# Retention and SwiGLU on one core: the q of jobs 4 to 7 turned by VectorE from blocks of 32 instead of by TensorE

## The chip, the cores and the metric

The kernel runs on one core of one Trainium2 chip. The metric is the device time of one execution in microseconds (us), the median of several runs. All values are float32.

## The reference

Two blocks follow each other. The first is a retention block (attention without softmax, with a decay that depends on the head), the second a feed-forward block with RMS norm and SwiGLU.

```python
batch, n_heads, seq, head_dim = (8, 8, 576, 64)
scores = scale * np.matmul(q, k.transpose(0, 1, 3, 2))
gamma = 1.0 - 2.0 ** (-5.0 - np.arange(H))
Dmat = np.where(rel >= 0, gamma[:, None, None] ** rel[None], 0.0)
attn = np.matmul(scores * Dmat[None], v)
x = attn.transpose(0, 2, 1, 3).reshape(4608, 512)
xn = x / np.sqrt(np.mean(x * x, axis=-1, keepdims=True) + 1e-06) * rms_g
g = xn @ w_gate                       # 512 x 1536
out = (g * (1 / (1 + np.exp(-g))) * (xn @ w_val)) @ w_out
```

## The kernel before

**Jobs.** The retention block is cut into 32 jobs: job `j` is one batch and one pair of heads (`jobs[j]`, numbered from 0; the words "jobs 5 to 8" of the change count from 1 and are jobs 4 to 7 here, all of batch 1). A job needs `qT` and `kT` (two heads x 64 dimensions on the 128 partitions, 576 positions along a row) and `k` and `v` with the positions on the partitions. A sequence of 576 is 4 full tiles of 128 positions and a tail of 64; the tails are loaded apart (`load_tails`, `TAILS`: heads 0 and 1, then heads 2 to 7, of batch 0 and of batch 1). Positions are worked in chunks of 64 (`L`).

**Steps of a job.** `T` is `turn` (make `qT` and `kT`), `V` is `scale_v` (decay factors on `v`), `S` is `slot`, which issues in this order: `values(j-1)` (product of weighed scores with `v`, line 379), `scores(j)` (292), `states(j)` (k times v per chunk, 315), `weigh` and `sums` (VectorE, lines 328 and 341), and `carried(j-1)` (the carried states times `qT`, 399, and the move of the finished result into `x`, lines 423 and 425). `C7` closes the last of the first eight jobs.

**The first eight jobs** (batches 0 and 1; `FIRST` = 8) run at the start of the kernel with little else to do for TensorE. In them both q and k are loaded with the positions on the partitions (`load_first`) and turned on TensorE: q by eight products with the identity (line 236), k by four transposes (230), the two tails by a transpose each (245). ScalarE copies the results out of PSUM (241, 252). The decay factor of q is applied late: VectorE multiplies it into the result on its way into `x` (425, table `gq`). **All later jobs** load q and k in blocks of 32 x 32 (`load_qk`, four DMAs for each), ScalarE scales q (line 259, table `gp`) and VectorE turns it with one instruction (264); their result is moved into `x` by ScalarE (423). In all jobs ScalarE scales `v` and its tail (273).

**The order is written out by hand.** Everything is issued in the order of the program text on each engine. `LOADS` lists the loads of the start; nearly all go to the DMA queue of SyncE (SP), some small ones to that of ScalarE (`act_table`, `act_tails`). Each load waits until the load eight before it has landed. `PLAN` is a list of steps: `T`, `V`, `S`, `C` as above; `Q` and `G` squares and their sums for the norm, `N`, `D`, `X` the norm of the first two blocks of 512 tokens; `w` and `a` steps of preparing the weights (VectorE and ScalarE: the weights are split into mantissa and exponent); `U` is `up_plain`, four products of 128x512 for tokens that are not yet done with combined weights (704); `P` and `F` prepare and fetch a later job; `W36` makes 36 halves of weights ready. From the first `U000` on, products of `up_plain` stand between all other steps, until the main loop over blocks of tokens begins.

The weights are prepared in `set_of(k)`, three rotating places inside the tile `ring`; the first `v`, `k` and `q` of batch 1 lie in the same tile.

The lines that matter to the order of a job:

```python
def slot(j, rest=True):
    if rest: values(j - 1)
    scores(j); states(j); weigh(j)
    if j < FIRST: sums(j)
    if rest: carried(j - 1)
```

and in `carried`, the move that depends on the kind of job:

```python
if j >= FIRST:
    nc.scalar.copy(out=o, in_=part)
    continue
nc.vector.tensor_tensor(out=o, in0=part, in1=gq..., op=ALU.mult)
```

In `values`, a one-element instruction on GpSimd (`tick`, line 386) stands between the last product of `values` and the first product of `carried`.

Of the kernel before, what the change touches and what calls it, by code (L numbers as in the profile page):

```python
# [10 lines left out]
F32 = mybir.dt.float32  # L11
U32 = mybir.dt.uint32
AF = mybir.ActivationFunctionType
ALU = mybir.AluOpType
P = 128
L = P // 2
SQ = 32
# [27 lines left out]
def kernel(  # L45
# [11 lines left out]
    nc = tc.nc  # L57
    B, H, S, D = q.shape
    NTOK, DM = out.shape
    DFF = moe_w_gate.shape[1]  # L60
    NHP = H // 2
    NF = DFF // P
    NC = S // L
    NFULL = S // P
    TAIL = S - NFULL * P
# [5 lines left out]
    NK = NH // 2  # L71
    NG = NH // 2
    FIRST = 2 * NHP
    EPS = 1e-6
    K0, K1 = 2.38924456, 0.703952253
    assert (D, DM, NHP * P) == (64, H * D, DM) and S % SQ == 0 and NTOK % U == 0
# [4 lines left out]
    raw = ctx.enter_context(tc.tile_pool(name="raw", bufs=1))  # L81
# [31 lines left out]
    gp = const.tile([P, NHP, 2], F32, name="gp")  # L113
# [37 lines left out]

    def load_qk(j):
        b, hp = jobs[j]
        for nm, src in (("q", q), ("k", k)):
            t = raw.tile([P, S // SQ, SQ], F32, tag=nm + "raw", name=f"{nm}raw_{j}")
            for e in range(2):
                rows = src[b, 2 * hp + e].rearrange("(t b) (i a) -> i b t a", b=SQ, a=SQ)
                for i in range(D // SQ):  # L160
                    r = e * D + i * SQ
                    nc.sync.dma_start(out=t[r : r + SQ], in_=rows[i])
            st[j][nm + "raw"] = t

    def load_first(j, nm):

        b, hp = jobs[j]
        n = NFULL * P
        at = (3 * hp + "qkv".index(nm)) * n
        room = (h_1.rearrange("p f t -> p (f t)") if b else flat_h)[:, at : at + n]  # L170
        src = {"q": q, "k": k, "v": v}[nm][b, 2 * hp : 2 * hp + 2, :n]
        if nm == "q":
            st[j]["q"] = room.rearrange("p (e t d) -> p e t d", e=2, d=D)
            nc.sync.dma_start(
                out=room.rearrange("p (e t) -> p e t", e=2),
                in_=src.rearrange("e (p t) d -> p e (t d)", p=P),
            )
            return
        t = st[j][nm] = room.rearrange("p (c e d) -> p c e d", e=2, d=D)
        for e in range(2):  # L180
            nc.sync.dma_start(out=t[:, :, e], in_=src[e].rearrange("(c p) d -> p c d", p=P))

    def load_tails(i, queue):

        b, heads = TAILS[i]
        for n, (nm, src) in enumerate((("qt", q), ("kt", k), ("vt", v))):
            at = NV + (3 * b + n) * DM
            t = vi[:TAIL, at : at + DM].rearrange("p (h d) -> p h d", d=D)
            cut = slice(heads[0], heads[-1] + 1)
            queue.dma_start(  # L190
                out=t[:, cut], in_=src[b, cut, NFULL * P :].rearrange("h p d -> p h d")
            )
            for hp in range(heads[0] // 2, heads[-1] // 2 + 1):
                st[b * NHP + hp][nm] = t[:, 2 * hp : 2 * hp + 2]
# [17 lines left out]
    def warm_up(n, width=P):  # L212
# [3 lines left out]
        for _ in range(n):  # L216
# [2 lines left out]
                start=True, stop=True,  # L219
            )  # L220

    def turn(j):

        d = st[j]
        n = NFULL
        for nm in "qk":
            ps = bank(f"turn_{j}_{nm}")
            for c in range(n):
                if nm == "k":
                    nc.tensor.transpose(  # L230
                        out=ps[:, c * P : c * P + P],
                        in_=d["k"][:, c].rearrange("p e d -> p (e d)"), identity=ident,
                    )
                    continue
                for e in range(2):
                    nc.tensor.matmul(
                        ps[side(e), c : n * P : n], lhsT=d["q"][:, e, c], rhs=ident,
                        start=True, stop=True,
                    )
            t = d[nm + "T"] = att.tile([P, S], F32, tag=nm + "T", name=f"{nm}T_{j}")  # L240
            nc.scalar.copy(out=t[:, : n * P], in_=ps[:, : n * P])
        last = bank(f"turn_{j}_t")
        for i, nm in enumerate("qk"):
            o = slice(i * TAIL, i * TAIL + TAIL)
            nc.tensor.transpose(
                out=last[:, o], in_=d[nm + "t"].rearrange("p e d -> p (e d)"),
                identity=ident[:TAIL, :TAIL],
            )
        warm_up(j == 0, 2 * P)
        for i, nm in enumerate("qk"):  # L250
            o = slice(i * TAIL, i * TAIL + TAIL)
            nc.scalar.copy(out=d[nm + "T"][:, NFULL * P :], in_=last[:, o])

    def prepare(j):

        d = st[j]
        for odd in range(2):
            t = d["qraw"][:, odd::2]
            nc.scalar.activation(
                out=t, in_=t, func=AF.Copy, scale=gp[:, jobs[j][1], odd : odd + 1]  # L260
            )
        for nm in ("q", "k"):
            t = att.tile([P, S], F32, tag=nm + "T", name=f"{nm}T_{j}")
            nc.vector.transpose(out=t, in_=d.pop(nm + "raw").rearrange("p t a -> p (t a)"))
            d[nm + "T"] = t
        scale_v(j)

    def scale_v(j):
        d = st[j]
        hp = jobs[j][1]  # L270
        for e in range(2):
            for t in (d["v"][:, :, e], d["vt"][:, e]):
                nc.scalar.activation(
                    out=t, in_=t, func=AF.Copy, scale=gv[: t.shape[0], hp, e : e + 1]
                )
# [115 lines left out]
    def carried(j):  # L391
# [15 lines left out]
        for u, c0, c1, o in ((b, 0, cut, b * L), (b + 1, cut, NC, 0)):  # L407
# [3 lines left out]
            for first in (c0, c0 + 1):  # L411
# [7 lines left out]
                for to, at in moves:  # L419
                    o = x[to, first - c0 :: 2]  # L420
                    part = av[odd][at, i * L : (i + n) * L].rearrange("p (c k) -> p c k", k=L)
                    if j >= FIRST:
                        nc.scalar.copy(out=o, in_=part)  # L423
                        continue
                    nc.vector.tensor_tensor(
                        out=o, in0=part, in1=gq[:, hp].unsqueeze(1).to_broadcast([P, n, L]),
                        op=ALU.mult,
                    )
# [722 lines left out]
    def store_blocks(n):  # L1151
# [4 lines left out]

    IN_PSUM = range(4, 36)
    PLAN = """
        T0 V0 a1 S0 a1 T1 a1 a1 V1 S1 T2 V2 F8 S2 V3 T3 w1 a1 w1 Q0 a1 a1 G0 Q1 a1 S3 T4 G1 V4
        a1 a1 w1 Q2 a1 S4 a1 V5 w1 T5 G2 V6 Q3 a1 a1 G3 a1 S5 w1 T6 V7 w1 Q4 a1 S6 N0 a1 w1 a1  # L1160
        D0 a1 a1 G4 a1 T7 a1 w1 a1 w1 a1 a1 a1 Q5 X0 G5 S7 w1 U000 w1 a1 a1 a1 Q6 a1 C7 G6 a1 Q7
        G7 U001 N1 w1 w1 w1 D1 U002 w1 a1 X1 a1 w1 a1 w1 w1 w1 w1 a1 a1 a1 w1 a1 U003 a1 w1 w1
        a1 U100 w1 a1 w1 U110 w1 a1 a1 w1 a1 w1 U101 a1 w1 w1 w1 a1 a1 a1 a1 a1 w1 U010 a1 U102
        a1 w1 a1 w1 w1 w1 U111 w1 U112 a1 a1 w1 w1 a1 a1 a1 w1 w1 a1 a1 w1 a1 U011 w1 U012 w1 w1
        a1 w1 a1 a1 U020 U021 w1 U103 w1 a1 a1 w1 w1 a1 a1 w1 w1 a1 U113 a1 w1 w1 a1 a1 a1 w1
        U013 a1 U022 a1 a1 a1 a1 w1 w1 a1 w1 U120 w1 a1 a1 a1 a1 a1 w1 U130 w1 w1 a1 a1 a1 U121
        a1 a1 a1 P8 a1 a1 w1 w1 a1 w1 U023 w1 U122 a1 F9 U123 w1 a1 w1 a1 w1 a1 a1 a1 w1 a1 w1
        w1 a1 a1 U030 U031 a1 a1 w1 w1 a1 a1 w1 a1 w1 U032 a1 U033 w1 U131 w1 w1 w1 w1 U132 a1
        w1 w1 P9 a1 a1 a1 a1 a1 a1 w1 w1 a1 U040 F10 a1 w1 a1 U133 w1 a1 U041 a1 a1 a1 w1 a1 a1
        U042 a1 w1 w1 w1 w1 w1 a1 a1 U050 w1 a1 a1 w1 a1 w1 a1 w1 w1 U051 U052 w1 w1 a1 w1 a1 a1  # L1170
        U140 w1 a1 a1 a1 w1 a1 w1 a1 a1 a1 w1 a1 U043 U053 W36 S8 P10 U141 S9 a1 U150 a1 U142
        F11 a1 a1 d0 a1 a1 Q8 z0 i0 a1 a1 U143 a1 S10 r1 a1 a1 U151 P11 U152 S11 U153 a1 d1 i1
        d2 a1 a1 a1 Q9 r2 A0 r99 A0 A0 j2 A0 G8 a1 a1 d3 b0 d4 C11 A0 i3 A0 d5 a1 A0 a1 F12 A0
        G9 b1 i4 Q10 k0 Q11 a1 b2 A0 i5 A0 a1 a1 G10 A0 j6 A0 A0 A0 a1 P12 A0 j7 b3 A0 j8 c2 A1
        c0 F13 A1 v1 A1 c3 A1 j9 o0 G11 A1 A1 j10 A1 A1 j11 A1 i12 A1 R2 A1 Y2 A1 X2 M2 p1 a1 a1
        i13 A1 A1 A1 A1
    """
    TAILS = ((0, range(2)), (0, range(2, H)), (1, range(2)), (1, range(2, H)))
    LOADS = [("k", 0), ("act_table", 2), ("q", 0), ("q", 1), ("q", 2), ("v", 0), ("k", 1), ("v", 1), ("tails", 1), ("q", 3), ("k", 2), ("act_table", 0), ("table", 3), ("half", 0), ("v", 2), ("v", 3), ("k", 3), ("v", 4), ("q", 4), ("k", 4), ("act_tails", 0), ("half", 1), ("tails", 2), ("k", 5), ("tails", 3), ("q", 5), ("v", 5), ("v", 6), ("q", 6), ("v", 7), ("k", 6), ("rms_g", 0), ("k", 7), ("q", 7), ("half", 2), ("half", 3), ("table", 4), ("half", 4)]
    stores = []  # L1180
    n_joined = 0
    due = False
# [160 lines left out]
```

## Time and profile before

| | |
|---|---|
| median of 3 runs | 1105.85 us (1105.76 to 1105.95) |
| the profiled execution's own time | 1103.84 us |
| its span, first to last instruction | 1102.0 us |
| TensorE (PE) busy | 1087.4 us, 99% of the span |
| VectorE (DVE), ScalarE (ACT), GpSimd (POOL) busy | 753.2, 339.5, 457.9 us |
| granted TensorE clock | 1.00 |

The profile names engines PE, PEld (its weight loads), DVE, ACT, POOL and SP. A float32 product appears as two records. A group line gives the source line, engine, operation, output<-inputs, shape and count, then busy time and mean duration in ns, then the idle time before these instructions and what ended it. "issue" as a releaser means that the profile shows nothing for which the engine waited. Times of day are microseconds from the start of the span.

### The profile page before, as it was taken

To read this page: it belongs to the slowest core of one execution; us is meant where nothing else is said; L and a number is where in the kernel's file an instruction comes from. 1 tells how busy PE (TensorE), PEld (TensorE's weight loads), DVE (VectorE), ACT (ScalarE), POOL (GpSimd) and SP (SyncE) were. 2 spreads that over 40 slices of the span, in tenths; PEclk is the share of its full clock that TensorE was granted. 3 is DMA by queue.
4 is the path that set the end of the run, shared out by engine and by line. 5 is a ranking of instruction groups with operands and counts; after the bars stand their busy time and mean duration, and the time that the engine had idled before them with its cause. 6 is when DMAs were issued, how large, how long until landed. Compare 5 with 4: busy or idle time off the path is not lost.

```text
span 1102.0 us, 24455 instructions
## 1 busy us (share of the span) xinstructions
PE 1087.4 (99%) x10102; PEld 912.5 (83%) x10102; DVE 753.2 (68%) x1219; ACT 339.5 (31%) x757; POOL 457.9 (42%) x421
## 2 busy tenths in 40 slices
PE   8899999999999999999999999999999999999998
PEld 7744444479988899889988998889888988898898
DVE  3878468878866794678667775668565935594467
ACT  5755564431124412342034303340233111211110
POOL 0027316548430195027702581238322942393236
PEclk9999999999999999999999999999999999999999
DMA  8856787696978876796678965888475855575461
GB/s 211 194 174 232 295 262 211 196 353 170 304 265 233 217 254 225 181 242 235 237 217 193 295 256 143 245 255 295 132 204 194 281 192 174 186 284 164 151 249 41
DMA packets 253871, 243.60 MB, mean 221 GB/s; under 512 B 193216, under 2 KB 213824, under 8 KB 247616
## 3 DMA queue, kind: packets, MB, share of 16 engines
q1 hardware_dynamic: 252320, 241.64, 69.3%
q8 instruction: 79, 1.29, 0.5%
q10 hardware_dynamic: 1440, 0.40, 0.2%
q14 instruction: 32, 0.26, 0.1%
HBM read 211.92 MB, written 30.08 MB: 220 GB/s over the span
## 4 chain that ended last, share of the span: by engine, by line
PE 96%; DVE 1%; DMA 1%; issue 1%; SPq 0%; ACT 0%; POOL 0%; POOLq 0%; DVEq 0%; ACTq 0%
PE up L704 15%; PE x L644 14%; PE w L644 13%; PE z L644 13%; PE y L644 7%; PE xo L814 6%; PE xp L814 4%; PE zo L814 4%; PE zp L814 3%; PE wo L814 2%; PE yo L814 2%; PE av L379 2%; PE wp L814 2%; PE av L399 2%; PE s L292 2%; PE yp L814 2%
## 5 line engine op out<-in xcount | busy, mean ns | idle before, releaser
L704 PE MATMUL up<-x,ring 128*128 128x512 f32 x384 | 167.1, 594 | 0.0
L644 PE MATMUL x<-x,ring 128*128 128x256 f32 x672 | 161.0, 382 | 0.0
L644 PE MATMUL w<-sums,ring 128*128 128x256 f32 x672 | 158.9, 379 | 0.0
L644 PE MATMUL z<-x,ring 128*128 128x256 f32 x672 | 158.7, 379 | 0.0
L766 POOL TENSOR_TENSOR vi<-h 128x384 f32<-128x384 f32 x32 | 39.9, 1247 | 275.3 <-DVE h L663 266.2
L704 PEld LDWEIGHTS up<-x,ring 128*128 128x128 f32 x384 | 72.2, 190 | 89.3 <-issue 84.7
L644 PEld LDWEIGHTS z<-x,ring 128*128 128x128 f32 x672 | 127.7, 190 | 19.9 <-issue 2.9
L644 PEld LDWEIGHTS w<-sums,ring 128*128 128x128 f32 x672 | 127.6, 190 | 17.4
L644 PEld LDWEIGHTS x<-x,ring 128*128 128x128 f32 x672 | 125.3, 190 | 17.5 <-ACT m L670 0.2
L771 POOL TENSOR_TENSOR vi<-h 128x384 f32<-128x384 f32 (+2 forms) x46 | 47.6, 1034 | 149.3 <-DVE h L663 149.3
L1010 POOL TENSOR_TENSOR vi<-vi 128x512 f32<-128x512 f32 (+1 forms) x77 | 78.1, 1027 | 38.2 <-DVE vi L841 21.5
L644 PE MATMUL y<-sums,ring 128*128 128x256 f32 x336 | 79.4, 379 | 0.0
L670 ACT COPY m<-x 128x512 f32<-128x512 f32 x42 | 24.6, 586 | 173.3 <-PE x L644 173.3
L651 DVE TENSOR_TENSOR h<-u,w 128x512 f32<-128x512 f32 x42 | 28.9, 688 | 67.8 <-PE w L644 67.8
L651 DVE TENSOR_TENSOR u<-m,y 128x512 f32<-128x512 f32 x42 | 28.8, 687 | 63.3 <-PE y L644 62.6
L644 PEld LDWEIGHTS y<-sums,ring 128*128 128x128 f32 x336 | 63.8, 190 | 8.7
L665 ACT ACTIVATE h<-h 128x512 f32<-128x512 f32 x63 | 39.7, 630 | 82.6 <-DVE h L651 82.6
L1130 POOL TENSOR_TENSOR vi<-vi 128x512 f32<-128x512 f32 (+1 forms) x24 | 40.7, 1696 | 30.7 <-DVE vi L1119 17.1
L651 DVE TENSOR_TENSOR u<-u,z 128x512 f32<-128x512 f32 x42 | 28.9, 688 | 33.5 <-PE z L644 33.4
L1130 POOL TENSOR_TENSOR ring<-ring 128x512 f32<-128x512 f32 x24 | 30.4, 1270 | 49.4 <-DMA w_up_blocks<-ring 43.7
L771 POOL TENSOR_TENSOR vi<-vi,h 128x384 f32<-128x384 f32 (+2 forms) x46 | 48.4, 1053 | 3.6
L423 ACT COPY x<-av 128x192 f32<-128x192 f32 (+6 forms) x136 | 37.7, 277 | 29.8 <-PE av L399 28.3
(314 smaller groups left out, 2087.3 us busy)
## 6 DMA issues: line engine op xcount, KB each, us to landing
ring<-w_out_blocks SPq DMA_DIRECT2D x59, 1344.0 KB, 6.7
ring<-w_up_blocks SPq DMA_DIRECT2D x42, 1792.0 KB, 7.7
w_out_blocks<-vi SPq DMA_DIRECT2D x21, 448.0 KB, 6.5
out_dram<-vi SPq DMA_DIRECT2D x64, 128.0 KB, 3.1
qraw<-in_q_dram SPq DMA_DIRECT2D x96, 72.0 KB, 4.8
kraw<-in_k_dram SPq DMA_DIRECT2D x96, 72.0 KB, 2.8
k<-in_k_dram SPq DMA_DIRECT2D x48, 128.0 KB, 2.8
v<-in_v_dram SPq DMA_DIRECT2D x48, 128.0 KB, 2.8
```

The costliest lines, as they stand in the source:

```text
L292: nc.tensor.matmul(s[e][side(odd), i * L : i * L + L], lhsT=d["kT"][side(e), c * L : c * L + L], rhs=d["qT"][side(e), c * L : c * L + L], ...
L423: nc.scalar.copy(out=o, in_=part)
L644: nc.tensor.matmul(ps[:, i * HU : i * HU + HU], lhsT=w[:, PLACE[blk], c, i * P : i * P + P], rhs=t_of[u][blk][:, c], start=(start and i == ...
L651: nc.vector.tensor_tensor(out=o, in0=a, in1=pairs_of(ps), op=ALU.add)
L665: nc.scalar.activation(out=o, in_=c, func=AF.Silu)
L670: nc.scalar.copy(out=s1, in_=pairs_of(x_))
L704: nc.tensor.matmul(ps, lhsT=w[:, PLACE[blk], c % 2, i * P : i * P + P], rhs=x_of[u][:, c], start=(c == 0), stop=(c == NHP - 1),)
L766: eng.tensor_tensor(out=i1, in0=x12, in1=x11, op=ALU.subtract)
L771: eng.tensor_tensor(out=o[:, c], in0=a[:, c], in1=b[:, c], op=op)
L814: nc.tensor.matmul(ps, lhsT=lhs[:, c], rhs=w[:, s, c], start=((nm, s // 4) not in first), stop=False, skip_group_check=True,)
L1010: eng.tensor_tensor(out=t[:, :, o], in0=t[:, :, x], in1=t[:, :, y], op=ALU.add)
L1130: nc.gpsimd.tensor_tensor(out=t[o], in0=t[x], in1=t[y], op=op)
```

## The change

For jobs 4 to 7, q is loaded by `load_qk` in blocks of 32 (into a free part of `ring`), scaled by ScalarE with `gp` and turned by VectorE (`turn_raw`); TensorE turns only k and its tail. The q tails of batch 1 are no longer loaded. The results of these jobs are moved into `x` by ScalarE without the factor `gq`. In all first eight jobs `qT` and `kT` become two halves of one tile, so that both tails are copied out of PSUM by one instruction; and the tails of `v` are scaled by four GpSimd instructions (one for each entry of `TAILS`) instead of 16 ScalarE instructions. `LOADS` and `PLAN` are written anew; `gp` moves to ScalarE's queue, `causal` and `gc` to SP's.

```diff
+    TURNED = range(4)
...
-    def load_qk(j):
+    def load_qk(j, names="qk"):
...
+            if j < FIRST:
+                at = AT_SETS + 4 * BLOCK * 3 - (FIRST - j) * S
+                t = ring[:, at : at + S].rearrange("p (t a) -> p t a", a=SQ)
...
     def load_first(j, nm):
+        if nm == "q" and j not in TURNED:
+            load_qk(j, "q")
+            return
...
     def load_tails(i, queue):
+            if nm == "qt" and b * NHP + heads[0] // 2 not in TURNED:
+                continue
...
+    def place_turned(j):
+        t = att.tile([P, 2, S], F32, tag="qkT", name=f"qkT_{j}")
+        st[j]["qT"], st[j]["kT"] = t[:, 0], t[:, 1]
+        return t
+
     def turn(j):
-        for nm in "qk":
+        both = place_turned(j)
+        names = "qk" if j in TURNED else "k"
+        if j not in TURNED:
+            turn_raw(j, "q")
+        for nm in names:
...
-        for i, nm in enumerate("qk"):
-            o = slice(i * TAIL, i * TAIL + TAIL)
-            nc.scalar.copy(out=d[nm + "T"][:, NFULL * P :], in_=last[:, o])
+        first = 2 - len(names)
+        nc.scalar.copy(
+            out=both[:, first:, NFULL * P :],
+            in_=last[:, : len(names) * TAIL].rearrange("p (i t) -> p i t", t=TAIL),
+        )
+
+    def turn_raw(j, names):
+        d = st[j]
+        if "q" in names:
+            for odd in range(2):
+                t = d["qraw"][:, odd::2]
+                nc.scalar.activation(
+                    out=t, in_=t, func=AF.Copy, scale=gp[:, jobs[j][1], odd : odd + 1]
+                )
+        for nm in names:
+            nc.vector.transpose(
+                out=d[nm + "T"], in_=d.pop(nm + "raw").rearrange("p t a -> p (t a)")
+            )
...
+    def scale_tails(b, heads):
+        cut = slice(heads[0], heads[-1] + 1)
+        t = vi[:TAIL, NV + (3 * b + 2) * DM : NV + (3 * b + 3) * DM]
+        t = t.rearrange("p (h d) -> p h d", d=D)[:, cut]
+        g = gv[:TAIL].rearrange("p h e -> p (h e)")[:, cut].unsqueeze(2)
+        nc.gpsimd.tensor_tensor(
+            out=t, in0=t, in1=g.to_broadcast([TAIL, len(heads), D]), op=ALU.mult
+        )
+
     def scale_v(j):
+        for b, heads in TAILS:
+            if (b, 2 * hp) == (jobs[j][0], heads[0]) and j < FIRST:
+                scale_tails(b, heads)
         for e in range(2):
-            for t in (d["v"][:, :, e], d["vt"][:, e]):
+            for t in (d["v"][:, :, e], d["vt"][:, e])[: 1 if j < FIRST else 2]:
...
-                    if j >= FIRST:
+                    if j not in TURNED:
                         nc.scalar.copy(out=o, in_=part)
...
-        T0 V0 a1 S0 a1 T1 a1 a1 V1 S1 T2 V2 F8 S2 V3 T3 w1 a1 w1 Q0 a1 a1 G0 Q1 a1 S3 T4 G1 V4
-        a1 a1 w1 Q2 a1 S4 a1 V5 w1 T5 G2 V6 Q3 a1 a1 G3 a1 S5 w1 T6 V7 w1 Q4 a1 S6 N0 a1 w1 a1
-        D0 a1 a1 G4 a1 T7 a1 w1 a1 w1 a1 a1 a1 Q5 X0 G5 S7 w1 U000 w1 a1 a1 a1 Q6 a1 C7 G6 a1 Q7
+        a1 V0 a1 a1 T0 S0 a1 T1 V1 S1 V2 T2 S2 T3 a1 w1 V3 a1 S3 a1 Q0 a1 G0 Q1 T4 a1 a1 V4 G1
+        w1 w1 a1 F8 a1 S4 Q2 a1 T5 V5 G2 V6 w1 Q3 G3 a1 a1 a1 a1 a1 S5 a1 w1 T6 w1 N0 a1 w1 Q4
+        w1 D0 S6 V7 T7 a1 a1 a1 Q5 X0 S7 G4 a1 a1 a1 a1 w1 Q6 a1 w1 a1 a1 U000 w1 a1 w1 G5 a1 C7
...
-    LOADS = [("k", 0), ("act_table", 2), ("q", 0), ("q", 1), ("q", 2), ("v", 0), ("k", 1), ("v", 1), ("tails", 1), ("q", 3), ("k", 2), ("act_table", 0), ("table", 3), ("half", 0), ("v", 2), ("v", 3), ("k", 3), ("v", 4), ("q", 4), ("k", 4), ("act_tails", 0), ("half", 1), ("tails", 2), ("k", 5), ("tails", 3), ("q", 5), ("v", 5), ("v", 6), ("q", 6), ("v", 7), ("k", 6), ("rms_g", 0), ("k", 7), ("q", 7), ("half", 2), ("half", 3), ("table", 4), ("half", 4)]
+    LOADS = [("k", 0), ("v", 0), ("q", 0), ("q", 1), ("table", 0), ("k", 1), ("v", 1), ("tails", 1), ("table", 2), ("q", 2), ("table", 3), ("v", 2), ("k", 2), ("v", 3), ("q", 3), ("k", 3), ("v", 4), ("k", 4), ("tails", 2), ("half", 0), ("q", 4), ("q", 5), ("half", 1), ("act_tails", 0), ("k", 5), ("v", 5), ("tails", 3), ("v", 6), ("q", 6), ("k", 6), ("half", 2), ("rms_g", 0), ("v", 7), ("k", 7), ("q", 7), ("half", 3), ("half", 4), ("act_table", 4)]
```

The rest of `PLAN` (the steps between `U001` and the main loop) holds the same `U`, `S`, `P`, `F`, `A` steps in another interleaving; of the inner sums, groups 2 and 6 move from VectorE to GpSimd and groups 3, 4 and 5 from GpSimd to VectorE.

## The prediction

> **What bounds the kernel now.** I read the engine totals first, then the windows on both sides of the first `up` product, then TensorE's groups and idle times in the early part, and last SP's queue.
>
> ```profile
> PE 1087.4 (99%) x10102; PEld 912.5 (83%) x10102; DVE 753.2 (68%) x1219; ACT 339.5 (31%) x757; POOL 457.9 (42%) x421
> ```
>
> TensorE is idle for only 14.6 us of 1102.0. Where these lie is told by two windows (columns: busy time of PE, PEld, DVE, ACT, POOL with counts, clock, DMA share, GB/s):
>
> ```profile
> 10.00:55.00 45.00, 38.98 (x1226) 33.48 (x1225) 33.05 (x87) 34.00 (x89) 1.64 (x8) 1.00 0.84 204
> 55.00:201.00 146.00, 145.72 (x415) 65.81 (x414) 105.41 (x182) 80.18 (x141) 59.58 (x43) 1.00 0.72 245
> ```
>
> Until 55 us (jobs 0 to 7, where the change lies) TensorE idles 6 us, DVE and ACT are three quarters busy and the DMA engines 84%: nothing bounds alone. From the first `up` at 55.05 us on TensorE never rests; after 195 us its waits add up to 1.6 us, and 4.3 us follow its last product. So **a change before 55 us is worth what it shifts the first `up`**, not what it takes off TensorE. In the early part, by shape, and TensorE's timeline at job 4:
>
> ```profile
> L236 PE MATMUL turn_q<-ident,ring 128*64 128x128 f32 x64 | 5.1, 281 | 2.9 <-issue 2.9
> ...
> L241 ACT COPY qT<-turn_q 128x512 f32<-128x512 f32 x8 | 4.7, 583 | 11.4 <-PE turn_q L236 11.4
> ```
> ```profile
> 27.47 0.65 PE L236 MATMUL turn_q<-ident,ring 128*64 128x128 f32 x6
> 29.71 0.81 PE L236 MATMUL turn_q<-ident,ring 128*64 128x128 f32 x10 [1.59 <-issue]
> ```
>
> The turn of q of jobs 4 to 7 is seen whole, with a pause of 1.59 us for which no wait is shown. SP's queue (start, duration, loads):
>
> ```profile
> 39.95 0.51 SPq L174 DMA_DIRECT2D ring<-in_q_dram  x1
> ...
> 43.27 3.93 SPq L162 DMA_DIRECT2D qraw<-in_q_dram  x4
> ```
>
> These are one q in the old and one in the new form: one issue against four. SP issues without a pause from 0.7 to 43 us. By the landing records q of job 7 lands at 43.98 us and is used at 47.4; q of job 5 lands at 34.98 and is used at 35.8. TensorE runs only 1 to 3 us behind the loads.
>
> **What the Trainium skill says.** "Runtime: NRT & Kernel Launch", section "Instruction fetch mechanics": instructions come in 16 KiB blocks by DMA, their cost "mostly hidden". Not here: packets of 16384 B start at 26.9 and 46.9 us, and TensorE pauses at 28.1 and 48.2; loads in flight land late too (in the gap around 31.8 us two successive landings are 2.85 us apart). "DMA: Bandwidth & Descriptors", table "Specifications": transfers under 512 B miss the line rate. The trace agrees: median packet 13 ns for 128 B, 18 for 256 B, 46 for 1024 B, so a byte of the new q costs 2.3 times a byte of the old. "GPSIMD Engine Reference", section 3.1: elementwise work is 1.96 times slower on GpSimd than on VectorE; here a 128x384 add takes 1.00 to 1.60 us against 0.55 to 0.86.
>
> **The change, step by step.** *TensorE:* eight q products per job are one stretch of 1.02 us (chain, jobs 5 and 6), the q tail half of 0.27: (1.02 + 0.13) x 4 = **4.6 us out**. That is the most the change can gain by its own work.
>
> *DVE:* out, the multiplies by `gq` of four jobs, four records and 0.94 us for each (first line, job 4), 3.8 us; in, four transposes of 128x576 (second line, of a later job):
>
> ```profile
> 42.01 0.94 DVE L425 TENSOR_TENSOR x<-av,gq 128x256 f32<-128x256 f32 x4
> ```
> ```profile
> L264 DVE STREAM_TRANSPOSE qT<-qraw 128x576 f32<-128x576 f32 x17 | 13.1, 772 | 0.7 <-PE av L399 0.7
> ```
>
> 4 x 0.77 = 3.1; net -0.7. *ACT:* out, four q copies (0.58), eight tail copies (0.22) and 16 tail scalings (0.34): 9.5 us. In, eight scalings
>
> ```profile
> L259 ACT ACTIVATE qraw<-qraw,gp 128x288 f32<-128x288 f32 x48 | 23.0, 530 | 8.5 <-DMA qraw<-in_q_dram 7.9 <-DVE sum L341 0.5
> ```
>
> 4.2, and 16 moves into `x`, 0.37 + 0.32 + 0.21 + 0.21 per job, 4.4: net -0.9. Neither engine is the bound; both small gains I count as nothing. *POOL:* four scalings, two 64x384 and two 64x128, by its own rows about 1.25 and 0.65 us. POOL is idle until 60 us (1.6 us busy), but behind such a scaling stands the `tick`, which releases `carried`. The late case is heads 2 to 7 of batch 1: v tail lands about 37.9 (ledger below), done 39.2, `carried(4)` due 39.4. Cost 0 to 0.5; I take 0.
>
> *Loads, the step that decides.* Old: four q of 256 packets of 1024 B (256 x 46 / 16 engines = 0.74 us) and 512 tail packets (0.58 in all): 3.5 us. New: 4 x 4 x 576 packets x 13 / 16 = 7.5 us. **4.0 us more** DMA time, and SP issues 16 q blocks for 4 q and 2 fewer tails. To see when it lands I add packet times in the order of `LOADS` and set landings of before against the sum: 20.4 landed at 27.7, 24.5 at 35.3, 28.7 at 39.9, 31.4 at 44.0, 34.1 at 47.3, 36.9 at 49.8 (job 8's first blocks, of the new kind). Instruction fetches are in these. In the new order the sums are: q4 20.4, q5 22.3, k5 24.8, last tails 26.4, q6 29.8, k6 31.0, k7 34.9, q7 36.7, so landings of about 27.7, 30.5, 35.5, 37.5, 42.2, 43.5, 48.4 and **49.7** against 43.98 for q7.
>
> TensorE behind it, with old durations: q4 27.7 + 1.06 + 0.77 = 29.5, so `scores(4)` at about 29.6 against 31.9, 2.3 ahead. k5 at 35.5 and the tails at 37.5 hold job 5: `carried(4)` ends 40.4 against 40.73. k6 at 43.5: turn 0.7, copies 0.8, scores, states and carried 2.0: 47.0 against 45.5. Norm 1.9, k7 turn 0.7, `rb` 1.05, values 0.67: 51.3. q7: 49.7 + 1.06 + 0.77 = **51.5**, which ends last. In before `scores(7)` at 52.62 stand 2.43 ahead of the first `up`; so 53.9 against 55.05, **-1.1 us**. Of 4.6 us, 3.5 turn into waits for loads.
>
> *The start:* q0 is issued behind v0, two issues, about +1.0; but `V0` moves ahead of the copies and `V1` no longer waits for its tail (states(1) idled 0.94 at 15.45): taken as 0, between -0.5 and +0.5. *After 55 us:* all products stay, in other order; groups 3 to 5 of inner sums go to DVE, 2 and 6 to POOL. Before has 0.7 us of waits between 200 and 260 us, so no gain beyond that; a plan that fits worse may cost up to 3. I take 0. The `ring` place of raw q lies under weight sets 1 and 2, the first of which is written after `x` of the second 512 tokens is normed, and its last reader is job 7's transpose.
>
> **Rivals.** (1) *The loads keep up*, nearly the whole 4.6 us is kept. For it: job 8's blocks landed 0.2 to 0.4 us apart, not 0.47, and fewer products mean fewer fetches. Against: other engines had been catching up behind a fetch. If 16 blocks take 0.3 each, q7 lands 2.7 earlier, 47.0; then k7 and TensorE's own order hold, first `up` near 51.5: -3.5, median **1102.3**. (2) *SP's queue becomes the bound, slower.* q7's last block is SP's 64th DMA, q7 was the 50th, issued at 39.95: 0.80 us each. At that rate it is issued at 51.1, lands 4.0 later at 55.1, first `up` at 55.1 + 1.83 + 2.43 = 59.4: +4.3, **1110.1**. It decides from a landing of q7 at 50.8 on. Against: 72 KB blocks free the eight places sooner, and part of the 0.80 is waiting for the engines. (3) *The new plan stalls TensorE after 55 us*, by +1 to +3: **1107**. (4) That the change does not do what it says: the instruction order of the changed kernel has 32 fewer q products, 4 fewer tail turns and 4 more transposes, so this has no weight.
>
> **How the numbers follow.** Against the profiled execution's 1103.84 the likeliest case gives 1102.7. The median is 2.0 higher; the same step there gives **1104.8**. About 0.2% (2.2 us) is what a measurement of this kernel can tell from no change. Main case, -2.2 to +2.2: 0.45. Loads keep up: 0.29 faster. SP's queue or the plan, beyond +2.2: 0.26. The range reaches from the full TensorE saving, less a little (-4.4, 1101.4), to most of the queue case (1109.5); its own range for the main case is 1103.6 to 1108.
>
> **What would show it.** TensorE's busy total near 1082.8. Idle before 55 us up from 6 to about 9.5 us, with waits for DMA (`kT`, tails) or for DVE's transpose ahead of jobs 5 to 7; a raw q7 landing of 49 to 51 us; first `up` near 53.9; no new waits after it. Wrong if q7 lands before 47.5 or after 52, if TensorE waits after 55 us grow beyond 1 us, or if ACT ends the waits early on.

## The result, and the profile after

The changed kernel takes 1108.02 us (median of 20 runs) beside 1104.96 for the kernel before on the same chip: ratio **1.0027, 95% interval 1.0016 to 1.0038**. It is slower by some 3 us, more than the 0.2% that the prediction set as a measurable difference; 1104.8 and "no change" were forecast. The profiled execution took 1106.24 us (before: 1103.84), its span is 1104.5.

The page gives the engine totals and the granted clock in 40 slices:

```profile
PE 1086.5 (98%) x10034; PEld 913.2 (83%) x10034; DVE 751.0 (68%) x1211; ACT 339.0 (31%) x753; POOL 452.7 (41%) x421
...
PEclk9699999999999999999999999999999999999999
```

TensorE issues 68 records of products fewer, yet its busy total is only 0.9 us lower, not 4.6: in the second slice (27.6 to 55.2 us) the clock stands at 6 tenths. The windows on both sides of the first `up` in the forecast (busy time of PE, PEld, DVE, ACT, POOL, then clock, DMA share, GB/s):

```profile
10.00:55.00 45.00, 38.14 (x1083) 33.39 (x1085) 30.42 (x77) 29.36 (x75) 3.64 (x11) 0.81 0.83 187
55.00:201.00 146.00, 145.72 (x502) 67.19 (x495) 108.23 (x181) 81.92 (x148) 59.75 (x43) 1.00 0.76 249
```

The clock was 1.00 in the first of these before, and is 0.81 now: the clock records show half rate from 30.2 to 43.85 us and from 47.27 to 50.68, in units of 3.413 us. The waits of TensorE (line, releaser: total, times, longest):

```profile
PE av L440 <- issue: 3.9, 3, 1.7
PE s L333 <- DVE qkT L286: 3.2, 2, 2.3
PE turn_q L257 <- DMA h<-in_q_dram: 2.6, 1, 2.6
PE av L420 <- issue: 1.9, 1, 1.9
```

and where they lie (start, busy, instructions, the idle time before them):

```profile
29.14 0.63 PE L420 MATMUL av<-ret,h 64*64 64x64 f32 x28 [1.92 <-issue]
32.27 1.34 PE L333 MATMUL s<-qkT 64*64 64x64 f32 x40 [2.34 <-DVE qkT L286]
37.24 0.91 PE L440 MATMUL av<-qkT,sum 64*64 64x64 f32 x12 [1.70 <-issue]
54.58 0.81 PE L333 MATMUL s<-qkT 64*64 64x64 f32 x40 [0.90 <-DVE qkT L286]
```

`scores` waits for VectorE's turned q at job 4 (32.27) and at job 7 (54.58). The clock record goes to half at 30.20 us, 1.06 us after the end of the pause of 1.92 and 0.27 us into the wait of 2.34. The products are slower then: the same 40 records take 1.34 us at 32.27 and 0.81 at 54.58. The second half-rate stretch, from 47.27 on, follows 3.4 us in which TensorE does not wait at all; over half of that time goes to sixteen records of one column each, of the norm:

```profile
44.90 1.95 PE L522 MATMUL ms<-mean_w,sq 128*128 128x1 f32 x16
```

The chain that ends in the first `up`:

```profile
49.66 1.48 PE av L440 x29
...
51.16 0.38 ACT x L464 x2
...
51.64 0.29 ACT x L464 x2
...
52.26 0.52 ACT ring L314
52.78 0.85 ACT ring L282 x2
...
53.66 0.79 DVE qkT L286
...
54.58 0.81 PE s L333 x40
...
55.86 0.93 PE av L440 x32
56.79 0.63 PE up L745
```

The last steps follow **ScalarE's order**: after `carried` of an earlier job come its moves into `x`, then the scaling of `v` (314), then that of q (282), then VectorE's turn, then `scores(7)`. Before, these jobs had neither the moves nor a scaling of q on ScalarE. But the wait that this order causes is 0.90 us, and the chain starts with a `carried` at half rate (1.48 us for 29 records). The first `up` stands at 56.72 us, against 54.98 before (the chain's figures, 56.79 here and 55.05 in the prediction, leave out what still overlaps with the work before).

By windows that end at the first `up`, TensorE was busy for 46.46 us and idle for 8.52 before; now it is busy for 46.02 and idle for 10.70. So the 1.74 us are 2.2 more of idle time (1.3 of it the longer wait for the first q) and only 0.4 less of busy time, though 4.6 us of work are gone.

**A sum that holds for every kernel here.** In each profile I take the time of the first `up`, add all gaps of TensorE over 0.05 us after it, and see what is left:

| profile | first `up` | idle after it | all else | span |
|---|---|---|---|---|
| before | 54.98 | 1.87 | 1045.2 | 1102.0 |
| after | 56.72 | 3.17 | 1044.6 | 1104.5 |

The difference of 2.5 us is 1.74 of a later first `up`, 1.30 of idle time after it, and -0.6 elsewhere. In the thirteen experiments "all else" lies between 1044.3 and 1045.5. Each row is one execution; ratios below are of the medians of many.

### The profile page after: what moved, and what is told of

The parts are those of the page before. It is cut to its first block, busy times and chain, and to the rows that moved or that the text cites. A ratio compares the mean times of both kernels' runs of the same rounds, so it can differ in the third digit from the quotient of the medians.

```text
span 1104.5 us, 24347 instructions
## 1 busy us (share of the span) xinstructions
PE 1086.5 (98%) x10034; PEld 913.2 (83%) x10034; DVE 751.0 (68%) x1211; ACT 339.0 (31%) x753; POOL 452.7 (41%) x421
## 4 chain that ended last, share of the span: by engine, by line
PE 95%; SPq 2%; DVE 1%; issue 1%; DMA 1%; ACT 0%; POOL 0%; POOLq 0%; ACTq 0%; DVEq 0%
PE up L745 15%; PE x L685 14%; PE w L685 13%; PE z L685 13%; PE y L685 7%; PE xo L855 6%; PE xp L855 4%; PE zo L855 4%; PE zp L855 3%; PE wo L855 2%; PE yo L855 2%; PE wp L855 2%; PE av L440 2%; PE av L420 2%; PE s L333 2%; PE yp L855 2%
## 5 line engine op out<-in xcount | busy, mean ns | idle before, releaser
L464 ACT COPY x<-av 64x64 f32<-64x64 f32 (+7 forms) x152 | 41.1, 280 | 33.8 <-PE av L440 32.4
L1171 POOL TENSOR_TENSOR ring<-ring 128x512 f32<-128x512 f32 x24 | 30.5, 1273 | 42.1 <-DVE ring L1160 32.6
```

The costliest lines, as they stand in the source:

```text
L1171: nc.gpsimd.tensor_tensor(out=t[o], in0=t[x], in1=t[y], op=op)
```

## The experiments

"After" and "before" are the two kernels. Clock means are over all timed runs: 0.9973 for before (48 runs), 0.9930 for after (20). Each ratio is to runs of before taken along with it, whose medians lie between 1104.96 and 1106.04 us; a range in brackets is its 95% interval.

### Is it the lists, or the new way of q?

Tails merged and on GpSimd, the old lists, all eight q turned on TensorE:

```diff
-    TURNED = range(4)
+    TURNED = range(8)
     # LOADS and PLAN of before, with gp on ScalarE's queue
```

> The changed kernel's code with TURNED = range(8) and the LOADS and PLAN of before (only the table gp on ScalarE's queue): what is left of the change is the merged tail copy and the v tails scaled by GpSimd. ScalarE loses 8 small copies and 16 small scalings (about 7 us). Expected by all theories: the same loads, no new wait, ratio 0.999 to 1.0005. If GpSimd's scaling holds up carried through the tick behind it, TensorE waits for POOL by 1 us or more in jobs 1 or 5 and the ratio is 1.001 to 1.003.

Measured: 1106.24 us, ratio 1.0006 (0.9998 to 1.0013). The tails alone cost nothing that can be told from no change, and no wait for GpSimd over 0.3 us appears.

The new lists, all eight q turned on TensorE (`TURNED = range(8)` alone):

> The changed kernel with TURNED = range(8): q of all eight jobs goes through TensorE again; the new LOADS and PLAN, the merged tail copy and the GpSimd tails stay. Theory clock (the q blocks make TensorE wait at job 4, the wait halves its clock from 30 to 44 us, and the halved stretches add to the late loads): q4 lands near 25 us in one DMA, no wait of 2.3 us before scores(4), clock 1.000, ratio to before 0.999 to 1.001. Theory loads (4.0 us more DMA work alone sets the end): the same ratio, so this run does not part these two. Theory lists (the new LOADS and PLAN are what costs): ratio stays 1.002 to 1.004.

1106.67 us, ratio 1.0013 (1.0006 to 1.0021), clock 0.9957: in none of the ranges. The new lists load q of job 4 later, and here TensorE waits for it:

```profile
PE turn_q L257 <- DMA ring<-in_q_dram: 3.1, 1, 3.1
```

By the point values the lists give away 0.7 thousandths against the old ones where TensorE turns q, and the other 1.4 of 1.0027 come with the new q; the intervals of neighbours overlap. Next, the new way of q with the lists of before:

> The changed kernel's code (q of jobs 4 to 7 turned by VectorE, merged tail copy, GpSimd tails) with the LOADS and PLAN of before, only the table gp moved from SP's queue to ScalarE's early on. Theory clock: TensorE waits for q blocks or k in jobs 4 to 7, 3 us or more in all, the clock falls in at least one stretch, ratio 1.002 to 1.006. Theory loads: waits but by their length alone, ratio 1.000 to 1.002 with clock 1.000. Theory lists: the 4.6 us are kept in part, ratio 0.996 to 0.999.

1112.21 us, ratio 1.0064 (1.0051 to 1.0077), clock 0.9915, just above the range of the theory of the clock. The old order puts the new q behind more work:

```profile
PE s L333 <- DVE qkT L286: 4.2, 2, 3.1
PE rb L587 <- ACT diag L536: 3.0, 1, 3.0
```

With the new q the new lists are no cost, but what keeps it at 1.0027. Then before itself, with `("q", 4)` moved behind `("k", 5)`, to see what a late q costs in the old form:

> The kernel before with one load moved: q of job 4 behind k of job 5 (landing near 31 instead of 25.4 us). No arithmetic and no number of loads is changed. Theory clock: TensorE waits some 3 us at the turn of job 4, its clock falls to half for 3.4 us or a multiple, mean clock 0.990 to 0.998, and the time grows by more than the first up would by the wait alone, ratio 1.002 to 1.005. Theory loads: a wait of 1 to 3 us, clock 1.000, the shift of the first up equals the wait or less because the loads run ahead again: ratio 1.000 to 1.002.

1106.94 us, ratio 1.0009 (0.9999 to 1.002), clock 0.9962. The wait for this q is 2.3 us in the profile, and by the medians less than half of it is seen in the time. That is the range of waits that cost their length or less; a wait that costs more than its length, as the theory of the clock had it, did not show here.

### Is it the blocks of q on the DMA queues?

After, with q of jobs 4 to 7 brought by one DMA each instead of four:

```diff
+            if j < FIRST:
+                nc.sync.dma_start(out=t.rearrange("p t a -> p (t a)"), in_=...)   # 128 rows of 2304 B
+                continue
```

> The changed kernel with q of jobs 4 to 7 loaded into the same place by one DMA each (128 rows of 2304 B, in the order of memory) instead of four in blocks of 32; the values that VectorE turns are then in the wrong order, all steps and sizes stay. It takes away the 4.0 us of extra DMA work and 12 of 16 issues. Theory late loads plus clock: q7 lands near 46 instead of 51.9 us, first up near 53 to 54 us, mean clock 0.997 or more, ratio to before 0.995 to 0.998, so that what the 4.6 us of TensorE work are worth without the blocks is seen. Rival (the loads are not what ends last; the order of the lists is): ratio 1.001 to 1.003.

The values of q stand in the wrong order in this kernel; steps and sizes are the same. 1105.9 us, ratio 1.0006 (0.9994 to 1.0018), clock 0.9941, between the ranges of the two theories. The loads are thus about 2 thousandths of the time (2.1, give or take 1.6). They are not the only thing that sets the first `up`: q of job 7 lands at 42.4 us here, against 51.87 in after, and `scores(7)` still waits. The chain of this run:

```profile
47.79 1.67 PE av L447 x32
...
49.48 0.83 ACT x L471 x4
50.31 0.80 ACT ring L321 x2
51.10 0.85 ACT ring L289 x2
...
51.98 0.79 DVE qkT L293
...
52.90 0.81 PE s L340 x40
```

With q landing 9.5 us earlier, `scores(7)` comes 1.7 us earlier and the first `up` stands at 55.05, no earlier than before. From the end of `carried` to the start of `scores(7)` there are 3.4 us of work on ScalarE and VectorE, one behind the other. `carried` itself was late: this run too has half rate, for 13.7 us before the first `up`.

### Is it the halved clock?

After, with 18 products of 128x256 that nobody reads, placed where TensorE waits: four ahead of the turn of k in jobs 5 and 6, seven ahead of `scores(4)`, three ahead of `scores(7)`.

```diff
+        for _ in range({4: 7, 7: 3}.get(j, 0)):          # in scores(j)
+            nc.tensor.matmul(s[2][:, 2 * P :], lhsT=ones, rhs=ones[:, :1].to_broadcast([P, 2 * P]), ...)
...
+            for _ in range({5: 4, 6: 4}.get(j, 0) if nm == "k" else 0):   # in turn(j)
```

> The changed kernel with products of 128x256 on constants added in TensorE's waits: four ahead of the turn of k in jobs 5 and 6, seven ahead of scores(4), three ahead of scores(7); they write PSUM columns that are overwritten or not read. Nothing else is changed. Theory clock: mean clock 0.997 or more, first up 1 us or more earlier than 56.8, ratio to before 0.999 to 1.001 against 1.0027 of the changed kernel. Theory loads: the clock recovers, but q7 still lands near 51.9 us and the first up stays at 56 to 57 us, ratio 1.002 to 1.003; the added products cost up to 2 us where nothing waits.

1104.14 us, ratio **0.9983 (0.9975 to 0.9991)**: faster than both kernels, with more work. The clock is 1.00 in the profile's first 60 us and 0.9979 over the runs. The mechanism that the theory named is not what the profile shows, though: the first `up` stands at 56.67, where it stood in after (56.72), q of job 7 lands at 52.51 here, and the 18 products take 8.9 us of TensorE. What the profile has less of is idle time behind the first `up`, 1.24 us for 3.17. With the seven products at job 4 alone:

> The changed kernel with only the seven added products ahead of scores(4), none at jobs 5 to 7. Theory clock (a wait that halves the clock costs more than its length): the first wait is the one that starts the long halved stretch (30 to 44 us), so most of the gain of all 18 products comes: mean clock about 0.996, ratio to before 0.999 to 1.001. Rival (any stretch with little work does it, jobs 5 to 7 as much): clock about 0.994 and ratio 1.001 to 1.0025.

1105.85 us, ratio 1.0003 (0.9992 to 1.0014), clock 0.9948: about half of the gain, with the ratio of the first theory and a clock nearer to that of the rival. The control, the same 18 products all just ahead of the first `up`, where TensorE does not wait:

> Control: the changed kernel with the same 18 products of 128x256, all ahead of the first up product, where TensorE does not wait for anything. Theory clock: they cost their own time, 18 x 0.3 = 5.4 us, and mend nothing: mean clock 0.993 as in the changed kernel, ratio to before 1.006 to 1.009. Rival (adding products changes something else, such as the instruction fetch or placement): ratio 1.004 or less.

1112.26 us, ratio 1.0061 (1.0045 to 1.0078), clock 0.9945: slower than after by 3.4 thousandths, as the theory of the clock had it. Products in general do not help; where they stand decides.

But a clock at full rate is not the whole of the gain. The same 18 products, one column wide instead of 256:

> The version with 18 added products in TensorE's waits, but each of one column (128x1) instead of 256: the same number of instructions at the same places, almost no work. Theory clock (the work in the waits keeps the clock up): the gain goes, mean clock 0.992 to 0.995, ratio to before 1.0015 to 1.003 as in the changed kernel. Rival fetch (the added instructions move the places where TensorE runs out of instructions, seen as idle time ended by issue: 6.2 us in the changed kernel's trace, 1.5 us with the 18 products): ratio 0.998 to 0.9995, issue waits of 1 to 3 us.

1105.27 us, ratio 1.0001 (0.9989 to 1.0012), and the clock stays at 0.9931, as in after. The clock is what the first theory expected, but more than half of the gain, which it expected to go, is kept. The windows of the first 60 us, first with 256 columns, then with one:

```profile
0.00:60.00 60.00, 53.50 (x1236) 43.91 (x1236) 36.20 (x94) 37.00 (x90) 4.72 (x18) 1.00 0.79 178
```
```profile
0.00:60.00 60.00, 51.97 (x1268) 44.46 (x1270) 36.26 (x96) 37.50 (x91) 4.75 (x18) 0.91 0.82 187
```

The group of seven takes as long in both, and yet the thin ones, with a weight load of 128x128 each, do not keep the clock up:

```profile
30.49 3.31 PE L335 MATMUL s<-ones 128*128 128x256 f32 x14
```
```profile
29.38 3.14 PE L335 MATMUL s<-ones 128*128 128x1 f32 x14
```

Of the 4.4 thousandths between after and the wide products, 2.6 come without any change of the clock and 1.8, about 2 us, together with it (each give or take 1.5). The pair of profiles does not show the second part: its execution with thin products is the fastest of 14 (1103.26 us), the one with wide products an average one (1104.19). What the runs show beyond it is that clock and time move together within one kernel: over 155 executions of before, the time falls by 0.55 us for each 0.001 of clock (correlation -0.67), over the 20 of after by 0.62 (-0.68). On that scale the 0.0043 of clock between before and after would be 2.4 to 2.7 of the 3 us. This is an estimate, and one of what goes together: a late load may both stretch the time and lower the clock.

**What halves the clock.** The clock records come in units of 3.413 us. For each unit that starts at full rate between 7 and 63 us, in the fifteen profiles, take the share in which TensorE was busy with products of more than one column. 26 such units were followed by half rate, and in all of them this share was 0.53 or less (0.36 for 26.79 to 30.20 in after). 171 were followed by full rate; two of them lie below that (0.47 in before, 0.48 in the control), the others at 0.54 or more. With the one-column products counted as busy there is no such line: ten of the 26 were then busy for 0.67 to 1.00, six of them without any gap. After's second stretch follows one of these six: it was busy throughout, and has 0.47 without the sixteen records of the norm. In before the same sixteen stand in the unit with 0.47 that stayed at full rate, so the share alone does not settle every case.

### What else came with 18 more products?

By the sum above, the thin products' profile has the first `up` at 55.88 (0.84 earlier than after) and 1.26 us of idle time after it, not 3.17. With wide products it is 1.24 us. This 1.9 us was a surprise, since no product stands there. The lines say which pauses are gone. After, two of them far into the kernel:

```profile
363.22 0.35 PE L440 MATMUL av<-qkT,sum 64*64 64x64 f32 x9 [1.45 <-issue]
```
```profile
814.12 0.33 PE L440 MATMUL av<-qkT,sum 64*64 64x64 f32 x4 [0.71 <-issue]
```

They recur in the two other kernels that issue the same number of products as after, the one with the old lists and the one with q in one piece (its lines shown), whose loads and order in the early part differ:

```profile
361.36 0.34 PE L447 MATMUL av<-qkT,sum 64*64 64x64 f32 x7 [1.25 <-issue]
```
```profile
812.70 0.33 PE L447 MATMUL av<-qkT,sum 64*64 64x64 f32 x3 [0.90 <-issue]
```

Counting TensorE's records from the start, those of products and those of weight loads (two of each for a product), these pauses stand at number 7038 to 7042 and 16192 to 16194 in all three kernels. In before and six of the others there is one at 6786 to 6788 instead. Early ones recur near 1200 (before, after, thin and wide products). A packet of 16384 B on the queue of instruction fetches starts 0.2 to 2.5 us ahead of most of them. So I tried to move the instructions alone: one-column products added to the warm-up at the very start.

```diff
         warm_up(6)
+        warm_up(16, 1)      # 32 in the second kernel
```

> The changed kernel with 16 products of 128 by 1 added to the warm-up at the very start, where TensorE waits 2.6 us for q of job 0 anyway. They do no work that anything uses; they only put every later TensorE instruction 32 records later. Theory A (a part of what the thin products brought came from where the instruction stream's own pauses fall): the pauses with no releaser, now at records 1200 and 1454, appear near the same record numbers and so some 32 records earlier in the work; the ratio leaves 1.0027 by over 0.001, to either side, with the mean clock still 0.992 to 0.994. Theory B (the thin products helped by breaking the waits at jobs 4 and 7): ratio 1.002 to 1.0035, nothing moves.

> The same with 32 products of 128 by 1 at the start, so that every later TensorE instruction is 64 records later. Theory A: the pauses stay near records 1200 and 1454 and fall 64 records earlier in the work; ratio away from 1.0027 by over 0.001 in this run or in that with 16, and the two differ; mean clock 0.992 to 0.994. Theory B: ratio 1.002 to 1.0035 as in the run with 16.

16: 1106.82 us, ratio 1.0009 (0.9999 to 1.0019), clock 0.9958. 32: 1114.8 us, ratio 1.0074 (1.0047 to 1.0102), clock 0.9950. As a pure shift both failed, since such a product takes 0.42 us in the warm-up. They outlast the wait for q, and the first turn starts 3.9 and 10.8 us later than in after; the clock moved too. The times therefore do not isolate the fetch. What does not depend on that is where the pauses fall. With 16, the first one is at number 948 and in the middle of a turn of q:

```profile
28.88 0.60 PE L257 MATMUL turn_q<-ident,h 128*64 128x128 f32 x6 [2.25 <-issue]
```

with 32 it is at number 950, inside `carried`. All work comes 64 records later there than with 16 (32 of products, 32 of weight loads), so a pause tied to the work would stand at 1012. After 60 us the first waits of TensorE read, in after and then with 16 products:

```profile
PE av L440 <- issue: 2.2, 2, 1.4
```
```profile
PE s L356 <- issue: 0.4, 1, 0.4
```

The pauses at 7038 and 16192 are gone, as in every kernel with another number of products. The pause of 0.4 us is of another kind: it stands at the same work, 208 to 219 us from the start, once in each of the fifteen profiles.

**The place of the others is tied to the count of instructions**, and more closely than these numbers say. If the records of TensorE's sequencer are counted too, the fifteen profiles have 57 further pauses without a releaser of more than 0.15 us, and every one of them ends at a record whose number, divided by 256, leaves 193 or 194. In each, a packet of 16384 B on the queue of instruction fetches had started 2.2 to 3.4 us (median 2.4) before the pause ended. After has 79 such packets and 20239 records, one packet for 256 records. No run here changes the fetch itself, but a pause at one place in 256 each time, at a fixed distance behind the packet, leaves little room for another cause. Not every such place has a pause; the work there decides. Behind 70 us, 20 of 22 stand among the 64x64 products of `values` and `carried`.

The run with 16 shows something more: a start that is 3.9 us later cost nothing by the medians (in the profile the first `up` is 2.9 us later and the idle time after it 2.1 us less; the ratio is 1.0009 against 1.0027).

### Two tries to do better

With the wide products, but q of job 7 in one piece turned on TensorE, which takes job 7's chain off ScalarE (`TURNED = (0, 1, 2, 3, 7)`, no products in `scores(7)`):

> The changed kernel with the added products (four each ahead of the turn of k in jobs 5 and 6, seven ahead of scores(4), none at job 7), and job 7's q loaded in one piece and turned on TensorE as in before: 1.0 us less DMA work ahead of scores(7), no ScalarE and VectorE step of 1.8 us there, 1.15 us more TensorE work. Theory clock plus late loads: q and k of job 7 land 1 us earlier, first up near 55.5 instead of 56.7, ratio to before 0.997 to 0.998 against 0.9983 of the version with all 18 products. Rival (q of job 7 is not what ends last): ratio 0.999 to 1.000, since 1.15 us of TensorE work come back.

1108.8 us, ratio 1.0031 (1.002 to 1.0042): a miss, outside both ranges. The clock stayed at 0.9975; q of job 7 landed at 48.9 us, but the first `up` came at 57.95, the pauses without a releaser add up to 4.9 us (1.5 with the wide products alone), and `states` waits for ScalarE's scaling of `v`:

```profile
PE s L344 <- ACT ring L320: 0.9, 1, 0.9
```

With the wide products, and one half-load of the weights, `("half", 2)`, moved behind q of job 7 so that this q lands earlier:

> The version with all 18 added products, and the third half of weights loaded behind q of job 7 instead of ahead of v of job 7, its three ScalarE steps two steps of PLAN later. Theory late loads: v, k and q of job 7 land 1.3 to 2 us earlier (q7 near 50.5), first up near 55.2 against 56.7, ratio to before 0.9965 to 0.998. Rival (the weights then are late and hold U002, or the gain is lost to the clock): ratio 0.998 to 1.001 with a wait of DVE or PE for the weights after 56 us.

1105.04 us, ratio 0.9999 (0.9988 to 1.0009): a miss as well. q of job 7 lands at 48.2 us and no wait is left ahead of `scores(7)`, yet the first `up` is at 57.46, not earlier than the 56.67 of the wide products alone. TensorE itself is what ends last here: from 10 us to the first `up` it is busy for 46.1 of 47.5 us. The added products, 8.9 us as in the wide kernel, no longer fill waits but cost their own time; those ahead of `scores(7)` run until 55.4, after VectorE's turn of q has ended (54.6):

```profile
53.81 1.57 PE L335 MATMUL s<-ones 128*128 128x256 f32 x6
```

## Why the prediction was wrong

**What held.** Waits for VectorE's transpose appeared ahead of `scores(4)` and `scores(7)`. They are 3.2 of the 6.9 us of idle time between 10 and 55 us; the rest are pauses without a releaser, and 9.5 had been forecast. The ledger of landings held within 2.1 us up to k of job 7: q4 29.75 (forecast 27.7), q5 31.9 (30.5), k5 35.4 (35.5), last tails 38.35 (37.5), q6 41.5 (42.2), k6 43.05 (43.5), k7 48.56 (48.4). SP's queue did not become the bound: the last block of q7 was issued at 47.87, not at 51.1. The start's wait for q0 grew by 1.3 us, where +1.0 was worked out and 0 taken. The busy total came to 1086.5 us, not to 1082.8. Of the signs of being wrong, one came true outright: waits after 55 us grew by more than 1 us.

**Step "q7: 49.7 + 1.06 + 0.77 = 51.5, which ends last".** Two terms failed. q7 landed at 51.87, 2.2 late; 2.3 us lie between the landings of its second and third block (49.20 and 51.50), and a packet of 16384 B of the instruction queue started at 48.89. And from there to `scores(7)` it took 54.58 - 51.87 = 2.7 us, not 1.83, as ScalarE reached q's scaling only after the moves and the scaling of `v`. Together that is 3.1 us: 51.5 becomes 54.58. With 2.14 us to the first `up`, not 2.43, this gives 56.72 where 53.9 was forecast. Correcting the landing alone would not have saved the step: with q7 at 42.4 us `scores(7)` still stood at 52.90, by ScalarE's chain behind a late `carried`. Nor would it have helped much to take away the wait for q7: the other path of the same sum, to the end of `values` at 51.3, ended at 53.68, so the wait for q7 is 0.90 us.

**Step "TensorE behind it, with old durations".** This term has no reason given, and it is the largest miss. The prediction set 4.6 us of work less against 3.5 us of waits more; up to the first `up` TensorE was busy for only 0.4 us less, while the idle time grew by 2.2. The rest of the 4.6 went into products at half rate, for 17.1 us of the profile: with the clock at full rate, in the wide kernel, the busy time without the added products is 41.3 us. The clock is not the only thing that holds the first `up`: with the clock at full rate it stood at 56.67 (wide products, q7 at 52.51), with early loads at 55.05 (one piece, half rate). No run has both without added products, so what 53.9 would have needed stays open.

**Step "Neither engine is the bound; both small gains I count as nothing".** This is the error behind the 0.9 us at job 7. I compared sums of busy time. ScalarE does lose work, but in before its copies of q stood behind TensorE's own product and could run as soon as that was done; now its scaling of q stands *ahead* of TensorE, in program order behind the moves of an earlier `carried`, which VectorE did before. At job 4 the same in small: q lands at 29.75, a square for the norm runs to 30.47, then q's scaling (0.86) and the turn (0.79) hold `scores(4)` until 32.27. 29.6 was forecast; of the 2.7 us, 2.05 are the late landing and 0.7 the square.

**Waits priced by their length alone.** What may follow a wait was put at nothing. "TensorE: Matmul & The Clock Gate" of the Trainium skill, in Part 1, "The HAM clock gate", states that the clock goes to half after an idle window of about 3.4 us and back after a busy one. The trace agrees with the two rates and the units of 3.413 us. It does not agree that the window has to be idle, nor with the rule of thumb under "Why this matters for your kernels", "No PE-idle gaps >~3µs": in the unit before the first halving TensorE was busy for 0.36, and its longest gap was 1.92 us. About 2 us of the time comes and goes with the clock (wide against thin products, by medians).

**Step "After 55 us ... I take 0".** Idle time after the first `up` rose by 1.30 us and the rest fell by 0.6. "A plan that fits worse" was the wrong reason to look for: two pauses of 1.45 and 0.71 us tied to the count of instructions stand there now, where before has one of 0.86; 68 records of products are gone, so that other work meets these places (79 packets were fetched in both kernels). The prediction cited "Instruction fetch mechanics" to doubt that fetches are hidden, and then did not ask where the pauses would fall after the change.

**Rivals.** The rival on the slow side, SP's queue, gave 1110.1 and "decides from a landing of q7 at 50.8 on". q7 did land later than that, and the sign of the change turned with it; but the issues were not late (47.87 for 51.1), so this rival is right by luck in its direction and wrong in its cause. None of the four rivals names ScalarE's order or the clock; ScalarE stands only among the signs of being wrong.

**What stays open.** How much of 2.6 thousandths with thin products is the shift of the pauses (1.9 us of idle time in one pair of profiles) and how much the earlier first `up` (0.84); why some pauses last 0.2 and others 3.3 us; how much of the 3 us is the clock, since the only runs at full rate have added work; what one-piece loads and a full clock together would give; and why the runs with 16 products are faster by median than their profile's sum says.

## What to carry to other kernels

When a step moves to an engine that is "only three quarters busy", place it in that engine's program order and follow the chain through it; the engine's total says nothing about that. When work on TensorE is traded for waits of 1 to 2 us each, look at the clock afterwards and do not take old durations over; wide products that nobody reads can fill such waits (here they turned 1.0027 into 0.9983, of which 1.8 thousandths went with the clock), but where no wait is left they cost their own time. And where a difference of 0.2% is in dispute, look first at the pauses without a releaser: adding or removing a few instructions changes which work they hit, and 1 to 2 us of difference may have nothing to do with the change's purpose.

## What the runs showed of the hardware that I had not expected

- The clock went to half after units of 3.413 us in which TensorE was busy for 0.53 or less with products of more than one column (26 of 26), six of them without any gap; in after it stayed at half from 30.20 to 43.85 us, although TensorE was busy for 6.0 of the 10 us from 30 to 40.
- Products of one column did not keep the clock up: seven of 128x1, which occupy TensorE for 3.14 us by the records, did not hold it (0.9931 over the runs), seven of 128x256 in 3.31 us did (0.9979), and sixteen records of the norm stand in the unit ahead of after's second halving, in which TensorE never waits.
- Pauses of TensorE without a releaser, 0.2 to 3.3 us long, end at one place in every 256 of its records (57 of 57 in fifteen profiles), 2.2 to 3.4 us after the start of a packet of 16384 B on the queue of instruction fetches.
